# A transformer kernel with a planned instruction order: new start, new bias matmuls, own buffer tag, a modelled store latency of 4 instead of 8

## Chip, cores, metric

One core of a Trainium2 chip (trn2). The metric is the device time of one execution in microseconds; quoted times are medians over several executions.

## The reference

Two layers; each is a local attention block and a feed-forward block, with the same weights in both layers. Input is 2048 tokens of width 1024, in bf16.

```python
for layer in (1, 2):
    x = x + A(layernorm(x), wqkv, wo)      # 32 heads of 32; each token attends to itself and 7 earlier ones, 2 apart
    x = x + B(layernorm(x), w1, b1, w2, b2)
# B: h = relu(x @ w1 + b1)**2, width 3584;  h @ w2 + b2
```

## The kernel before

The tokens of each layer are processed as four units of 512, so there are units 0 to 7. A unit goes through these stages (names of tiles in brackets): layernorm to a transposed, normalised input (`xnA`); projections q, k, v (`pq`); attention, mostly on VectorE (products `P`, logits `lg` on TensorE, exponentials `e`, denominator `dn`, result `o`); output projection (`py`), residual (`xm`), second layernorm (`xnB`); feed-forward 1 and 2. Units 1 to 7 do the two feed-forward products with a Strassen-type scheme of 7 products instead of 8: feed-forward 1 as 256-wide matmuls into `X`, `Y`, `Z`, feed-forward 2 as 512-wide ones. It needs sums and differences of weight blocks. Unit 0 does its products plainly, forms these combinations on VectorE on the side (tiles `tv`) and stores them in DRAM (`w1s`, `tw`) for the others.

No instruction is issued where the program text stands. Every operation is put into a plan with a modelled duration, a priority and its dependencies; a list scheduler runs the plan against modelled engines, buffer classes and a modelled DMA rate, and the order in which it starts operations is the fixed order of each engine's queue.

```python
LAT, PE_SLACK, DMA_LAT, DMA_MBS = 0.25, 0.3, 2.2, 0.36      # the model's constants
class Plan:
    def schedule(self):
        # ... an operation is picked when its engine is free, its inputs are done, and for every new buffer
        # a slot of its class is free and the number of live buffers of that tag is under its cap:
        if b.tag in self.caps and (live.get(b.tag, 0) >= self.caps[b.tag] or b.idx != placed.get(b.tag, 0)):
            ok = False
        # ... a DMA ends at max(dma_free, end) + MB / DMA_MBS, plus op.lat
p.caps.update(w=5, xnA=1, xnB=1, tv=4, T=1, ...)             # one xnA alive at a time

def SA(self, u):                                             # load x, layernorm, transpose
    xnT = Buf("8K", "xnA", [128, 4, self.KD, 128], F16)
    after = [self.state[u - 2].get("gatev")] if u >= 2 else ()
    ...
def keep_w2(self, j0, n, w):                                 # combinations of w2, stored for units 1..7
    p.add("DVE", ..., 45.0, name="tv")
    self.dma(..., prio=50.0, name="twst", lat=8.0)           # keep_w1 likewise
def SW(self, u):                                             # output projection, residual, second layernorm
    ... self.ln(xm, ..., vec=False, on_pe=(u in (0, self.NU - 1)))    # vec: statistics on VectorE
def SF2(self, u):                                            # seven products; b2 is added by matmul, 2 per product:
    mul("B21", *block(1, 0), Y, True, 0); ... mul("T1", ..., Z, True, 1); ... mul("T4", *block(1, 1), X, False, 0)
```

The softmax here doesn't subtract the row's maximum and nothing guards it: scores larger than these inputs give would overflow.

Of the kernel before, what the change touches and what calls it, by code (L numbers as in the profile page):

```python
# [8 lines left out]
BF = mybir.dt.bfloat16  # L9
# [16 lines left out]
DMA_LAT = 2.2  # L26
DMA_MBS = 0.36


def dve(n, fast=True):  # L30
    return 0.15 + n * (0.000523 if fast else 0.00104)
# [177 lines left out]
class _Kernel:  # L209
# [19 lines left out]
    def setup(self):  # L229
# [22 lines left out]
        with nc.allow_non_contiguous_dma(reason="tiny bias load"):  # L252
            nc.gpsimd.dma_start(self.b1T[:], self.b1.rearrange("(c p) -> p c", p=128))
        self.b2r = const.tile([128, D], BF, name="b2r")
        nc.gpsimd.dma_start(self.b2r[:], self.b2.rearrange("(o d) -> o d", o=1).to_broadcast((128, D)))
        self.row0 = const.tile([128, 128], F16, name="row0")
        nc.vector.memset(self.row0[:], 1.0)
        nc.gpsimd.affine_select(out=self.row0[:], in_=self.row0[:], pattern=[[0, 128]], compare_op=ALU.is_equal,
                                fill=0.0, base=0, channel_multiplier=1)

# [24 lines left out]
        p.classes["ps"] = (8, 2048)  # L285
        p.caps.update(w=5, xt=2, P0=4, P1=4, pr=2, pb=2, dn=1, e=1, xm=6, xnA=1, xnB=1, xn=2, xo=2, q=1, k=1, v=1, o=1, r2=1, s1=1, tv=4, T=1, wl=2)

# [34 lines left out]
    def keep_w2(self, j0, n, w):  # L322
        nc, p = self.nc, self.p
        t = [Buf("2K", "tv", [128, 2, BLK], F16) for _ in range(4)]

        def raw(k2, n2):
            return w[:, k2, :n, n2 * BLK:(n2 + 1) * BLK]

        def comb(i, a, b, r):
            p.add("DVE", dve(n * BLK), lambda: nc.vector.tensor_tensor(t[i][:, :n], a(), b(), ALU.subtract), r, [(t[i], 0)], 45.0, name="tv")  # L330
            self.dma(lambda: self.tw[i][:, j0:j0 + n, :], lambda: t[i][:, :n], [(t[i], 0)], [(("tw", i), j0)], n * 0.13, prio=50.0, name="twst", lat=8.0)
        comb(0, lambda: raw(0, 1), lambda: raw(0, 0), [(w, 0)])
        comb(1, lambda: raw(1, 1), lambda: t[0][:, :n], [(w, 1), (t[0], 0)])
        comb(2, lambda: raw(1, 1), lambda: raw(0, 1), [(w, 0), (w, 1)])
        comb(3, lambda: raw(1, 0), lambda: t[1][:, :n], [(w, 1), (t[1], 0)])
# [30 lines left out]
    def add_b2(self, bank, n2, start):  # L366
        self.nc.tensor.matmul(bank[:], self.row0[:], self.b2r[:, n2 * BLK:(n2 + 1) * BLK], start=start, stop=False, skip_group_check=True)

# [34 lines left out]
    def keep_w1(self, dp, w):  # L403
        nc, p = self.nc, self.p
        at = {pr: i for i, (d, pr) in enumerate(self.order1) if d == dp}

        def raw(m, k):
            return w[:, m, 4 * k:4 * k + 4, :]

        def store(pr, src, r, cast=None):  # L410
            i = at[pr]
            self.dma(lambda: self.w1s[i // 4][:, i % 4], src, r, [(("w1s", i // 4), i % 4)], 0.26, prio=50.0, name="w1st", cast=cast, lat=8.0)
        s1, s3, s2, s4 = t = [Buf("2K", "tv", [128, 4, 256], F16) for _ in range(4)]

        def comb(t, a, b, op, r, pr):
            p.add("DVE", dve(1024), lambda: nc.vector.tensor_tensor(t[:], a(), b(), op), r, [(t, 0)], 45.0, name="tv")
            store(pr, lambda: t[:], [(t, 0)])
        comb(s1, lambda: raw(1, 0), lambda: raw(1, 1), ALU.add, [(w, 1)], 5)
        comb(s3, lambda: raw(0, 0), lambda: raw(1, 0), ALU.subtract, [(w, 0), (w, 1)], 7)
        comb(s2, lambda: s1[:], lambda: raw(0, 0), ALU.subtract, [(w, 0), (s1, 0)], 6)  # L420
        comb(s4, lambda: raw(0, 1), lambda: s2[:], ALU.subtract, [(w, 0), (s2, 0)], 3)
# [76 lines left out]
    def ln_first(self, x, xv, xnT, tl):  # L498
# [3 lines left out]
        st = Buf("H", "st", [128, D // 512, nc.vector.BN_STATS_DIM], F32)  # L502
        mv, lnv, rstd, nmr = (lambda: sm[:, 0:2]), (lambda: sm[:, 2:3]), (lambda: sm[:, 3:4]), (lambda: sm[:, 4:5])
        pr = self.nxt()
# [9 lines left out]

        def f3():
            nc.vector.scalar_tensor_tensor(out=nmr(), in0=sm[:, 0:1], scalar=-1.0, in1=rstd(), op0=ALU.mult, op1=ALU.mult)

        def f4():
            nc.scalar.activation(out=xn[:], in_=xv(), func=ACTF.Identity, bias=nmr(), scale=rstd())

        p.add("DVE", 1.6, f1, [(x, 0)], [(sm, 0), (st, 0)], -1e5 + pr, name="bn")
        p.add("ACT", 0.5, f2, [(sm, 0)], [(sm, 1)], -1e5 + pr, name="bn2")
        p.add("DVE", 0.15, f3, [(sm, 0), (sm, 1)], [(sm, 2)], -2e5 + pr, name="bn3")
        p.add("ACT", 1.05, f4, [(x, 0), (sm, 1), (sm, 2)], [(xn, 0)], -1e5 + pr, name="bn4")
        self.transpose(xn, xnT, tl, -1e5 + pr)

    def transpose(self, xn, xnT, tl, prio):
        nc, p, KD = self.nc, self.p, self.KD
        pt = Buf("ps", "pt", [128, KD, 128], F16)

        def f5():
            for kd in range(KD):
                nc.tensor.transpose(pt[:, kd, :], xn[:, kd * 128:(kd + 1) * 128], self.ident[:])

        def f6():
            nc.vector.tensor_copy(xnT[:, tl], pt[:])
        p.add("PE", 1.0, f5, [(xn, 0)], [(pt, 0)], prio, name="pt")
        p.add("DVE", 0.69, f6, [(pt, 0)], [(xnT, tl)], prio - 200.0, name="ptc")

# [11 lines left out]
    def SA(self, u):  # L551
        layer, b = divmod(u, self.NB)
        st = self.state.setdefault(u, {})
        xnT = Buf("8K", "xnA", [128, 4, self.KD, 128], F16)
        st["xnA"] = xnT
        after = [self.state[u - 2].get("gatev")] if u >= 2 else ()
        for tl in range(4):
# [7 lines left out]

    def SQ(self, u, jobs, order=None):
        nc, p = self.nc, self.p
# [22 lines left out]
        for nm, c0 in order:  # L590
# [3 lines left out]
            def fm(pq=pq, w=w, c0=c0):  # L594
                for kd in range(KD):
                    wv = w[kd // 4][:].rearrange("p (a b) n -> p a (b n)", a=4)
                    nc.tensor.matmul(pq[:], wv[:, kd % 4, c0:D:8], xnT[:, :, kd, :], start=(kd == 0), stop=(kd == KD - 1))  # L597
            st["gate" + nm] = self.pe(8, fm, [(xnT, i) for i in range(4)] + [(w[0], 0), (w[1], 0)], [(pq, 0)], name="pq")
            p.add("ACT", act(512), lambda dst=dst, c0=c0, off=off, pq=pq: nc.scalar.copy(dst[:, c0, off:off + BLK], pq[:]),  # L599
                  [(pq, 0)], [(dst, c0)], 2.0, name="cast")  # L600
            yield
# [106 lines left out]
    def SW(self, u):  # L708
# [8 lines left out]
        for tl in range(4):  # L717
# [3 lines left out]
            for db in range(D // 512):  # L721
# [7 lines left out]
                def fe(py=py, xm=xm, xv=xv, db=db):  # L729
# [4 lines left out]
            self.ln(xm, lambda xm=xm: xm[:], [0, 1], xnT, tl, lambda t=t: self.xnd[2 * layer + 1][t * 128:(t + 1) * 128, :],  # L734
                    (("xnd", 2 * layer + 1, t), 0), 1.0, False, on_pe=(u in (0, self.NU - 1)))

    def SF1_plain(self, u):
# [6 lines left out]
        for dp in range(self.NDP):  # L744
# [4 lines left out]
            for m in range(2):  # L749
                for a in range(2):  # L750
# [4 lines left out]
                    def fm(ph=ph, w=w, m=m, a=a):  # L755
                        for kd in range(KD):
                            nc.tensor.matmul(ph[:], w[:, m, kd, a * 128:(a + 1) * 128], xnT[:, :, kd, :], start=(kd == 0), stop=(kd == KD - 1))  # L757

                    def fr(ph=ph, r=r, f=f):
                        nc.scalar.activation(out=r[:], in_=ph[:], func=ACTF.Relu, bias=self.b1T[:, f:f + 1], scale=1.0)  # L760

                    def fs(r=r, f=f):
                        nc.scalar.activation(out=r2[:, f, :], in_=r[:], func=ACTF.Square)
                    self.pe(8, fm, [(xnT, i) for i in range(4)] + [(w, m)], [(ph, 0)], name="ph")
                    p.add("ACT", 0.69, fr, [(ph, 0)], [(r, 0)], 2.0, name="relu")
                    p.add("ACT", 0.63, fs, [(r, 0)], [(r2, (f, 0)), (r2, (f, 1))], 1.9, name="sq")
# [93 lines left out]
    def SF2(self, u):  # L860
# [35 lines left out]
        def block(k2, m2):  # L896
            return (lambda jj, q: r2[:, k2 * h + jj, m2 * HB + q * 128:m2 * HB + (q + 1) * 128]), (lambda j0: cells(k2, m2, j0))
# [9 lines left out]
        X, Y, Z = bank("X"), bank("Y"), bank("Z")  # L907
        mul("B11", *block(0, 0), X, True)
        for q in range(2):
            add(X[q], q, 0)  # L910
        for j0 in (0, g):
            comb(lambda j0=j0: blk(0, 0, j0), lambda j0=j0: s1[:, j0:j0 + g, :], lambda j0=j0: blk(0, 0, j0), ALU.subtract,
                 cells(0, 0, j0) + [(s1, j0)], cells(0, 0, j0))
        mul("B21", *block(1, 0), Y, True, 0)
        for q in range(2):
            self.out_tile(layer, b * 4 + q, 0, Y[q], xm[q])
        for j0 in (0, g):
            comb(lambda j0=j0: blk(1, 0, j0), lambda j0=j0: blk(1, 0, j0), lambda j0=j0: blk(0, 0, j0), ALU.subtract,
                 cells(1, 0, j0) + cells(0, 0, j0), cells(1, 0, j0))
        mul("T1", lambda jj, q: s1[:, jj, q * 128:(q + 1) * 128], lambda j0: [(s1, j0)], Z, True, 1)  # L920
        for q in range(2):
# [8 lines left out]
        for q in range(2):  # L930
            self.out_tile(layer, b * 4 + q, 1, Z[q], xm[q])
        mul("T4", *block(1, 1), X, False, 0)
        for q in range(2):
# [14 lines left out]
    def run(self, a, b=(), pace=1):  # L948
# [4 lines left out]
        for _ in b:  # L953
            pass

    def build(self):
        self.setup()
        NU = self.NU
        NCH = self.NCH
        self.SA(0)  # L960
        order = []
        for c0 in range(NCH - 2):
            order += [("k", c0), ("q", c0)]
        order += [("k", NCH - 2), ("k", NCH - 1), ("q", NCH - 2), ("q", NCH - 1)]
        self.run(self.SQ(0, "kq", order))
        self.run(self.SQ(0, "v"))
# [70 lines left out]
```

## Time and profile before

The five runs before the prediction had a median of 1237.2 us (1235.9 to 1240.0).

| | before |
|---|---|
| span of the profiled run | 1235.2 us |
| TensorE busy / VectorE busy | 1191.3 us (96%) / 1023.7 us (83%) |
| matmul work: all matmuls of the program at the spacing below | 1174.6 us |
| span up to the end of the last matmul, less that work | 57.1 us |
| of it before unit 1's feed-forward 1 (the "head") | 41.3 us |

Busy time is a poor gauge here. The Trainium skill ("Trainium Kernel Development and Optimization", Performance Expectations) says that matmul busy time is a bad metric because matmuls are pipelined. The trace agrees: matmuls 512 columns wide start 0.2157 us apart but each is recorded as 0.379 us long. So I count matmuls in the built program (0.2157 us for 512 columns, 0.109 for 256, 0.0558 for 128, the spacings of undisturbed stretches), and call what an interval takes beyond that count its *cost*: idle time, half-rate clock and pipeline ends.

From the page of before (busy time and share; busy tenths of 40 slices of 30.9 us; granted TensorE clock in tenths):

```profile
PE 1191.3 (96%) x6832; PEld 741.1 (60%) x6874; DVE 1023.7 (83%) x1553; ACT 676.5 (55%) x1240; POOL 4.3 (0%) x11
...
PE   6987999899999999999999999999999998999998
...
PEclk9998999999999999999999999999999999999999
```

Counted from 1, TensorE is busy for less than 90% of slices 1, 3, 4 and 8, all in the first 250 us, and of slices 34 and 40. The timeline of TensorE before shows the early gaps (start, duration, operation, matmuls in the group, and in brackets the idle time before it and what ended it):

```profile
14.25 7.36 PE L597 MATMUL pq<-xnA,w 128*128 128x512 f16 x20 [0.78 <-DVE xnA L536]
22.22 6.26 PE L597 MATMUL pq<-xnA,w 128*128 128x512 f16 x28 [0.61 <-DMA w<-in_A_wqkv_dram]
28.32 1.89 PE L645 MATMUL lg<-P,grp 128*128 128x512 f16 x8
...
88.67 12.05 PE L597 MATMUL pq<-xnA,w 128*128 128x512 f16 x48 [3.70 <-ACT k L599]
...
110.69 0.39 PE L726 MATMUL py<-w,o 128*128 128x512 bf16 x1 [1.77 <-DVE o L695]
113.34 4.02 PE L726 MATMUL py<-w,o 128*128 128x512 bf16 x9 [2.27 <-DVE o L695]
119.39 1.04 PE L533 MATMUL pt<-ident,xn 128*128 128x128 f16 x8 [2.03 <-ACT xn L450]
...
241.21 1.03 PE L597 MATMUL pq<-xnA,w 128*128 128x512 f16 x4
248.18 15.12 PE L597 MATMUL pq<-xnA,w 128*128 128x512 f16 x60 [5.95 <-DMA w<-in_A_wqkv_dram]
```

A group's duration also shows the clock. At full rate 9 matmuls take 9 x 0.2157 + 0.17 (the end of the last) = 2.1 us; at 113.34 they took 4.02, so the array ran at half rate after the wait. The long waits shown here, at 88, 110 to 120 and 248 us, are therefore each paid twice.

The wait at 88.67 names a cast on ScalarE (ACT), and ScalarE's own timeline shows why it was late: an operation that needs VectorE's denominator stood ahead of the casts in ScalarE's in-order queue.

```profile
87.28 0.42 ACT L675 ACTIVATE dn<-dn 128x256 f32<-128x256 f32 x1 [15.51 <-DVE dn L672]
87.73 0.42 ACT L676 ACTIVATE ri<-dn 128x256 bf16<-128x256 f32 x1
88.05 3.00 ACT L599 CAST k<-pq 128x512 f16<-128x512 f32 x6
```

The wait at 248.18 is a weight load. The timeline of the DMA-issuing queue (SP) shows that its second half was issued only at 240.96, just as TensorE got there, behind stores of combinations (`tw`) and results (`xs`):

```profile
231.50 0.40 SPq L302 DMA_DIRECT2D w<-in_A_wqkv_dram  x1
236.08 1.18 SPq L302 DMA_DIRECT2D xs<-xo  x2
...
239.34 1.52 SPq L302 DMA_DIRECT2D tw<-tv  x3
240.96 0.44 SPq L302 DMA_DIRECT2D w<-in_A_wqkv_dram  x1
```

### The profile page before, as it was taken

To read this page: it belongs to the slowest core of one execution; us is meant where nothing else is said; L and a number is where in the kernel's file an instruction comes from. 1 tells how busy PE (TensorE), PEld (TensorE's weight loads), DVE (VectorE), ACT (ScalarE), POOL (GpSimd) and SP (SyncE) were. 2 spreads that over 40 slices of the span, in tenths; PEclk is the share of its full clock that TensorE was granted. 3 is DMA by queue.
4 is the path that set the end of the run, shared out by engine and by line. 5 is a ranking of instruction groups with operands and counts; after the bars stand their busy time and mean duration, and the time that the engine had idled before them with its cause. 6 is when DMAs were issued, how large, how long until landed. Compare 5 with 4: busy or idle time off the path is not lost.

```text
span 1235.2 us, 17952 instructions
## 1 busy us (share of the span) xinstructions
PE 1191.3 (96%) x6832; PEld 741.1 (60%) x6874; DVE 1023.7 (83%) x1553; ACT 676.5 (55%) x1240; POOL 4.3 (0%) x11
## 2 busy tenths in 40 slices
PE   6987999899999999999999999999999998999998
PEld 3653544356855578456874658545784555844863
DVE  5799999837999899994989999894889999997562
ACT  6533895048851689119870488506982173752640
POOL 1000000000000000000000000000000000000000
PEclk9998999999999999999999999999999999999999
DMA  9685978798899688987989688897799946688964
GB/s 308 194 213 161 295 243 255 237 347 258 334 325 361 212 317 288 366 327 222 347 281 366 232 290 315 301 362 248 247 356 344 347 161 217 245 286 320 344 235 170
DMA packets 209239, 348.29 MB, mean 282 GB/s; under 512 B 67136, under 2 KB 133952, under 8 KB 196352
## 3 DMA queue, kind: packets, MB, share of 16 engines
q1 hardware_dynamic: 197984, 333.22, 79.9%
q10 hardware_dynamic: 7488, 13.63, 2.9%
q0 software_dynamic: 3680, 0.28, 0.5%
q8 instruction: 54, 0.88, 0.3%
q14 instruction: 33, 0.27, 0.1%
HBM read 292.56 MB, written 46.40 MB: 274 GB/s over the span
## 4 chain that ended last, share of the span: by engine, by line
PE 73%; DVE 16%; DMA 5%; ACT 4%; issue 1%; SPq 1%; ACTq 0%; DVEq 0%
PE pq L597 18%; PE X L833 13%; PE X L887 11%; PE Z L833 7%; PE Z L887 5%; PE py L726 5%; DVE pr L690 4%; PE py L358 4%; PE Y L833 3%; DMA w<-in_B_w_dram 3%; PE Y L887 2%; DMA w<-in_A_wqkv_dram 2%; DVE pr L693 2%; PE ph L757 2%; PE lg L645 2%; DVE pr L694 1%
## 5 line engine op out<-in xcount | busy, mean ns | idle before, releaser
L597 PE MATMUL pq<-xnA,w 128*128 128x512 f16 x1536 | 344.5, 384 | 11.0 <-DMA w<-in_A_wqkv_dram 6.6
L597 PEld LDWEIGHTS <-w 128*128 128x128 bf16 x1536 | 220.8, 144 | 130.4 <-issue 13.6
L833 PEld LDWEIGHTS <-w 128*128 128x128 f16 (+1 forms) x2544 | 248.9, 98 | 36.5 <-issue 1.5
L887 PEld LDWEIGHTS <-r 128*128 128x128 f16 x1176 | 114.8, 98 | 140.1 <-issue 5.8
L630 DVE TENSOR_TENSOR P<-q,k 128x2048 f16<-128x2048 f16 x128 | 152.7, 1223 | 51.5 <-ACT q L599 51.5
L887 PE MATMUL X<-w,r 128*128 128x512 f16 (+1 forms) x777 | 176.2, 379 | 1.3 <-DVE xm L893 1.0
L690 DVE TENSOR_TENSOR pr<-pb,v 128x2048 f16<-128x2048 f16 x128 | 156.5, 1223 | 1.0 <-DVE pb L679 0.5
L599 ACT CAST k<-pq 128x512 f16<-128x512 f32 x64 | 37.0, 588 | 196.1 <-PE pq L597 195.2
L833 PE MATMUL X<-T,w 128*128 128x256 f16 x1104 | 134.1, 273 | 1.3 <-ACT u L807 1.3
L638 DVE TENSOR_TENSOR P<-P,P 128x2048 f16<-128x2048 f16 x99 | 120.9, 1222 | 2.2
L726 PE MATMUL py<-w,o 128*128 128x512 bf16 x496 | 114.8, 386 | 5.0 <-DVE o L695 4.0
L821 ACT ACTIVATE r<-rr 128x1024 f16<-128x1024 f16 x98 | 102.0, 1057 | 10.2 <-DVE rr L817 8.1
L807 ACT CAST u<-X 128x512 f16<-128x512 f32 x147 | 83.9, 586 | 39.7 <-PE X L833 37.6
L693 DVE TENSOR_TENSOR pr<-pr 128x1024 f16<-128x1024 f16 x128 | 88.2, 689 | 3.1
L726 PEld LDWEIGHTS <-o 128*128 128x128 bf16 x512 | 50.8, 99 | 66.0 <-DVE o L695 4.8
L810 DVE TENSOR_TENSOR rr<-u,Z 128x512 f16<-128x512 f16 x98 | 65.6, 683 | 23.4 <-PE Z L833 14.2
L475 ACT ACTIVATE xn<-xm 128x1024 f16<-128x1024 f32 x32 | 33.9, 1058 | 80.9 <-DVE xm L731 72.4
L731 DVE TENSOR_TENSOR xm<-py,xt 128x512 f32<-128x512 f32 x64 | 43.4, 687 | 30.5 <-PE py L726 25.8
L675 ACT ACTIVATE dn<-dn 128x256 f32<-128x256 f32 x16 | 6.6, 416 | 109.1 <-DVE dn L672 108.7
L694 DVE TENSOR_TENSOR pr<-pr 128x512 f16<-128x512 f16 x128 | 54.4, 425 | 4.4
L817 DVE TENSOR_SCALAR rr<-rr,b1T 128x256 f16<-128x256 f16 (+1 forms) x196 | 51.0, 315 | 1.0
L358 PE MATMUL py<-w,r 128*128 128x512 bf16 x219 | 49.4, 379 | 0.3
(100 smaller groups left out, 1346.8 us busy)
## 6 DMA issues: line engine op xcount, KB each, us to landing
w<-w1s SPq DMA_DIRECT2D x78, 1024.0 KB, 8.7
w<-tw SPq DMA_DIRECT2D x56, 896.0 KB, 8.9
w<-in_A_wqkv_dram SPq DMA_DIRECT2D x48, 1024.0 KB, 8.5
w<-in_B_w_dram SPq DMA_DIRECT2D x42, 896.0 KB, 7.2
w<-in_A_wo_dram SPq DMA_DIRECT2D x16, 1024.0 KB, 8.5
xt<-xs SPq DMA_DIRECT2D x32, 512.0 KB, 8.7
w<-in_B_w_dram SPq DMA_DIRECT2D x28, 512.0 KB, 6.9
xs<-xo SPq DMA_DIRECT2D x32, 256.0 KB, 6.8
```

What stands on the lines that cost most here:

```text
L358: nc.tensor.matmul(bank[:], r2[:, k2 * h + j0 + j, tl * 128:(tl + 1) * 128], w[:, k2, j, n2 * BLK:(n2 + 1) * BLK], start=False, stop=(j0 + ...
L597: nc.tensor.matmul(pq[:], wv[:, kd % 4, c0:D:8], xnT[:, :, kd, :], start=(kd == 0), stop=(kd == KD - 1))
L630: nc.vector.tensor_tensor(cur[:], q[:, c, None, hb * HB:(hb + 1) * HB].to_broadcast([128, W, HB]), _win_ap(k[:, c, :], HALO + hb * HB, HB) ...
L638: nc.vector.tensor_tensor(other[:], other[:], cur[:], ALU.add)
L690: nc.vector.tensor_tensor(pr[:], pb[:], _win_ap(v[:, c, :], HALO + hb * HB, HB), ALU.mult)
L693: nc.vector.tensor_tensor(pr[:, 0:4, :], pr[:, 0:4, :], pr[:, 4:8, :], ALU.add)
L694: nc.vector.tensor_tensor(pr[:, 0:2, :], pr[:, 0:2, :], pr[:, 2:4, :], ALU.add)
L726: nc.tensor.matmul(py[:], o[:, c, tl * 128:(tl + 1) * 128], wos[c // 4][:].rearrange("p (a b) n -> p a (b n)", a=4)[:, c % 4, db * 512:(db ...
L807: p.add("ACT", act(512), lambda: nc.scalar.copy(us[i][:], X[:]), [(X, 0)], [(us[i], 0)], 1.0, name="u")
L821: p.add("ACT", act(1024), lambda: nc.scalar.activation(out=r2[:, f:f + 2, :].rearrange("p a t -> p (a t)"), in_=r[:].rearrange("p a m t -> ...
L833: nc.tensor.matmul(bank[:, a, :], lw[:, k, a * 128:(a + 1) * 128], rhs(k), start=(start and k == 0 and a == 0), stop=(k == 3), skip_group_ ...
L887: nc.tensor.matmul(banks[q][:], left(jj, q), w[:, j, :], start=(start and jj == 0 and b2 is None), stop=(jj == h - 1), skip_group_check=True)
```

## The change

Its intent is to fill TensorE's gaps in the head and to drop superfluous bias matmuls. It has seven parts; the names in capitals are mine. The diff is cut to its core.

```diff
 # RATE
-DMA_MBS = 0.36
+DMA_MBS = 0.38
 # B2: the b2 row enters through the product that feeds all four outputs, and a difference where needed
-        mul("B11", *block(0, 0), X, True)
+        mul("B11", *block(0, 0), X, True, 0)
-        mul("B21", *block(1, 0), Y, True, 0)
+        mul("B21", *block(1, 0), Y, True)
-        mul("T1", ..., Z, True, 1)
+        mul("T1", ..., Z, True, "d")
-        mul("T4", *block(1, 1), X, False, 0)
+        mul("T4", *block(1, 1), X, False)
+        # b2 as two rows, loaded, not broadcast to 128; selector matrices pick[0], pick[1], pick["d"]=pick[1]-pick[0]
 # CAP
-        p.caps.update(w=5, ...)
+        p.caps.update(pk=2, lg=4, w=5, ...)
 # STORE
-   keep_w2: self.dma(..., name="twst", lat=8.0)
+   keep_w2: self.dma(..., name="twst", lat=4.0)
-   keep_w1: self.dma(..., name="w1st", lat=8.0);  p.add("DVE", ..., 45.0, name="tv")
+   keep_w1: self.dma(..., name="w1st", lat=4.0);  p.add("DVE", ..., self.nxt(), name="tv")
 # START (ln_first, transpose, SQ of unit 0, build)
-            nc.scalar.activation(out=xn[:], in_=xv(), func=ACTF.Identity, bias=nmr(), scale=rstd())
+            nc.vector.tensor_scalar(out=xn[:], in0=xv(), scalar1=sm[:, 0:1], scalar2=rstd(), op0=ALU.subtract, op1=ALU.mult)
+        (nc.scalar.copy if act else nc.vector.tensor_copy)(xnT[:, tl], pt[:])     # act for two of four tiles
+            # the first 3 k projections as two 256-wide halves each, order k k k, then q and k in turn
+        self.keep_clock(11, self.p.ops[0])      # 11 dummy 512-wide matmuls (pk), lowest priority
 # TAG (SA)
-        xnT = Buf("8K", "xnA", [128, 4, self.KD, 128], F16)
+        xnT = Buf("8K", "xnA1" if u == 1 else "xnA", [128, 4, self.KD, 128], F16)
-        after = [self.state[u - 2].get("gatev")] if u >= 2 else ()
+        after = [self.state[max(u - 2, 1)].get("gatev")] if u >= 2 else ()
 # SPLIT (SW and plain feed-forward 1 of unit 0)
-     self.ln(xm, ..., False, on_pe=(u in (0, self.NU - 1)))
+     self.ln(xm, ..., u == 0 and tl >= 2, on_pe=(u in (0, self.NU - 1)))
+     # the first two ph outputs as two 256-wide halves each, the first needing only token tiles 0 and 1
```

More of the change, by code (lines that the diff above doesn't have):

```diff
@@ L253, in setup @@
             nc.gpsimd.dma_start(self.b1T[:], self.b1.rearrange("(c p) -> p c", p=128))
-        self.b2r = const.tile([128, D], BF, name="b2r")
-        nc.gpsimd.dma_start(self.b2r[:], self.b2.rearrange("(o d) -> o d", o=1).to_broadcast((128, D)))
-        self.row0 = const.tile([128, 128], F16, name="row0")
-        nc.vector.memset(self.row0[:], 1.0)
-        nc.gpsimd.affine_select(out=self.row0[:], in_=self.row0[:], pattern=[[0, 128]], compare_op=ALU.is_equal,
-                                fill=0.0, base=0, channel_multiplier=1)
+        self.b2r = const.tile([128, BLK], BF, name="b2r")
+        nc.vector.memset(self.b2r[:], 0.0)
+        for n2, row in enumerate((32, 0)):
+            nc.gpsimd.dma_start(self.b2r[row:row + 1, :], self.b2.rearrange("(o d) -> o d", o=1)[:, n2 * BLK:(n2 + 1) * BLK])
+        self.pick = {}
+        for n2, row in enumerate((32, 0)):
+            t = self.pick[n2] = const.tile([128, 128], BF, name=f"pick{n2}")
+            nc.vector.memset(t[:], 1.0)
+            nc.gpsimd.affine_select(out=t[:], in_=t[:], pattern=[[0, 128]], compare_op=ALU.is_equal,
+                                    fill=0.0, base=-row, channel_multiplier=1)
+        t = self.pick["d"] = const.tile([128, 128], BF, name="pickd")
+        nc.vector.tensor_tensor(t[:], self.pick[1][:], self.pick[0][:], ALU.subtract)
         self.wqkv_v = self.wqkv.rearrange("(kt p) n -> p kt n", p=128)
@@ L285, in setup @@
         p.classes["ps"] = (8, 2048)
-        p.caps.update(w=5, xt=2, P0=4, P1=4, pr=2, pb=2, dn=1, e=1, xm=6, xnA=1, xnB=1, xn=2, xo=2, q=1, k=1, v=1, o=1, r2=1, s1=1, tv=4, T=1, wl=2)
+        p.caps.update(pk=2, lg=4, w=5, xt=2, P0=4, P1=4, pr=2, pb=2, dn=1, e=1, xm=6, xnA=1, xnB=1, xn=2, xo=2, q=1, k=1, v=1, o=1, r2=1, s1=1, tv=4, T=1, wl=2)
     def place(self, b):
@@ L330, in comb @@
             p.add("DVE", dve(n * BLK), lambda: nc.vector.tensor_tensor(t[i][:, :n], a(), b(), ALU.subtract), r, [(t[i], 0)], 45.0, name="tv")
-            self.dma(lambda: self.tw[i][:, j0:j0 + n, :], lambda: t[i][:, :n], [(t[i], 0)], [(("tw", i), j0)], n * 0.13, prio=50.0, name="twst", lat=8.0)
+            self.dma(lambda: self.tw[i][:, j0:j0 + n, :], lambda: t[i][:, :n], [(t[i], 0)], [(("tw", i), j0)], n * 0.13, prio=50.0, name="twst", lat=4.0)
         comb(0, lambda: raw(0, 1), lambda: raw(0, 0), [(w, 0)])
@@ L366, in add_b2 @@
     def add_b2(self, bank, n2, start):
-        self.nc.tensor.matmul(bank[:], self.row0[:], self.b2r[:, n2 * BLK:(n2 + 1) * BLK], start=start, stop=False, skip_group_check=True)
+        self.nc.tensor.matmul(bank[:], self.pick[n2][:], self.b2r[:], start=start, stop=False, skip_group_check=True)
     def w2_rhs(self, name, half):
@@ L411, in store @@
             i = at[pr]
-            self.dma(lambda: self.w1s[i // 4][:, i % 4], src, r, [(("w1s", i // 4), i % 4)], 0.26, prio=50.0, name="w1st", cast=cast, lat=8.0)
+            self.dma(lambda: self.w1s[i // 4][:, i % 4], src, r, [(("w1s", i // 4), i % 4)], 0.26, prio=50.0, name="w1st", cast=cast, lat=4.0)
         s1, s3, s2, s4 = t = [Buf("2K", "tv", [128, 4, 256], F16) for _ in range(4)]
         def comb(t, a, b, op, r, pr):
-            p.add("DVE", dve(1024), lambda: nc.vector.tensor_tensor(t[:], a(), b(), op), r, [(t, 0)], 45.0, name="tv")
+            p.add("DVE", dve(1024), lambda: nc.vector.tensor_tensor(t[:], a(), b(), op), r, [(t, 0)], self.nxt(), name="tv")
             store(pr, lambda: t[:], [(t, 0)])
@@ L502, in ln_first @@
         st = Buf("H", "st", [128, D // 512, nc.vector.BN_STATS_DIM], F32)
-        mv, lnv, rstd, nmr = (lambda: sm[:, 0:2]), (lambda: sm[:, 2:3]), (lambda: sm[:, 3:4]), (lambda: sm[:, 4:5])
+        mv, lnv, rstd = (lambda: sm[:, 0:2]), (lambda: sm[:, 2:3]), (lambda: sm[:, 3:4])
         pr = self.nxt()
@@ L513, in f2, with transpose @@
             nc.scalar.activation(out=rstd(), in_=lnv(), func=ACTF.Exp, scale=-0.5)
-        def f3():
-            nc.vector.scalar_tensor_tensor(out=nmr(), in0=sm[:, 0:1], scalar=-1.0, in1=rstd(), op0=ALU.mult, op1=ALU.mult)
         def f4():
-            nc.scalar.activation(out=xn[:], in_=xv(), func=ACTF.Identity, bias=nmr(), scale=rstd())
-        p.add("DVE", 1.6, f1, [(x, 0)], [(sm, 0), (st, 0)], -1e5 + pr, name="bn")
-        p.add("ACT", 0.5, f2, [(sm, 0)], [(sm, 1)], -1e5 + pr, name="bn2")
-        p.add("DVE", 0.15, f3, [(sm, 0), (sm, 1)], [(sm, 2)], -2e5 + pr, name="bn3")
-        p.add("ACT", 1.05, f4, [(x, 0), (sm, 1), (sm, 2)], [(xn, 0)], -1e5 + pr, name="bn4")
-        self.transpose(xn, xnT, tl, -1e5 + pr)
-    def transpose(self, xn, xnT, tl, prio):
+            nc.vector.tensor_scalar(out=xn[:], in0=xv(), scalar1=sm[:, 0:1], scalar2=rstd(), op0=ALU.subtract, op1=ALU.mult)
+        p.add("DVE", 1.55, f1, [(x, 0)], [(sm, 0), (st, 0)], -1e5 + pr, name="bn")
+        p.add("ACT", 0.55, f2, [(sm, 0)], [(sm, 1)], -1e5 + pr, name="bn2")
+        p.add("DVE", 0.5, f4, [(x, 0), (sm, 0), (sm, 1)], [(xn, 0)], -2e5 + pr, name="bn4")
+        self.transpose(xn, xnT, tl, -1e5 + pr, act=tl % 2 == 0)
+    def transpose(self, xn, xnT, tl, prio, act=False):
         nc, p, KD = self.nc, self.p, self.KD
@@ L535, in f6 @@
         def f6():
-            nc.vector.tensor_copy(xnT[:, tl], pt[:])
+            (nc.scalar.copy if act else nc.vector.tensor_copy)(xnT[:, tl], pt[:])
         p.add("PE", 1.0, f5, [(xn, 0)], [(pt, 0)], prio, name="pt")
-        p.add("DVE", 0.69, f6, [(pt, 0)], [(xnT, tl)], prio - 200.0, name="ptc")
+        p.add("ACT" if act else "DVE", 1.05 if act else 0.69, f6, [(pt, 0)], [(xnT, tl)], prio - 200.0, name="ptc")
     def load_x(self, layer, t, after=(), prio=None, tag="xt"):
@@ L564, in SA, with SQ @@
                         (("xnd", 2 * layer, t), 0), 20.0, False)
-    def SQ(self, u, jobs, order=None):
+    def SQ(self, u, jobs, order=None, split=0):
         nc, p = self.nc, self.p
@@ L597, in fm, with fh @@
                     nc.tensor.matmul(pq[:], wv[:, kd % 4, c0:D:8], xnT[:, :, kd, :], start=(kd == 0), stop=(kd == KD - 1))
-            st["gate" + nm] = self.pe(8, fm, [(xnT, i) for i in range(4)] + [(w[0], 0), (w[1], 0)], [(pq, 0)], name="pq")
+            if split:
+                def fh(n2, pq=pq, w=w, c0=c0):
+                    for kd in range(KD):
+                        wv = w[kd // 4][:].rearrange("p (a b) n -> p a (b n)", a=4)
+                        nc.tensor.matmul(pq[:, n2 * HB:(n2 + 1) * HB], wv[:, kd % 4, c0:D:8], xnT[:, 2 * n2:2 * n2 + 2, kd, :],
+                                         start=(kd == 0 and n2 == 0), stop=(kd == KD - 1), skip_group_check=True)
+                for n2 in range(2):
+                    self.pe(4, lambda fh=fh, n2=n2: fh(n2), [(xnT, 2 * n2), (xnT, 2 * n2 + 1), (w[0], 0), (w[1], 0)], [(pq, n2)],
+                            prio=self.nxt() + 3.0 * n2, name="pq")
+                split -= 1
+            else:
+                st["gate" + nm] = self.pe(8, fm, [(xnT, i) for i in range(4)] + [(w[0], 0), (w[1], 0)], [(pq, 0), (pq, 1)], name="pq")
             p.add("ACT", act(512), lambda dst=dst, c0=c0, off=off, pq=pq: nc.scalar.copy(dst[:, c0, off:off + BLK], pq[:]),
-                  [(pq, 0)], [(dst, c0)], 2.0, name="cast")
+                  [(pq, 0), (pq, 1)], [(dst, c0)], 2.0, name="cast")
             yield
@@ L734, in SW @@
             self.ln(xm, lambda xm=xm: xm[:], [0, 1], xnT, tl, lambda t=t: self.xnd[2 * layer + 1][t * 128:(t + 1) * 128, :],
-                    (("xnd", 2 * layer + 1, t), 0), 1.0, False, on_pe=(u in (0, self.NU - 1)))
+                    (("xnd", 2 * layer + 1, t), 0), 1.0, u == 0 and tl >= 2, on_pe=(u in (0, self.NU - 1)))
     def SF1_plain(self, u):
@@ L757, in fm, with fh @@
                             nc.tensor.matmul(ph[:], w[:, m, kd, a * 128:(a + 1) * 128], xnT[:, :, kd, :], start=(kd == 0), stop=(kd == KD - 1))
+                    def fh(n2, ph=ph, w=w, m=m, a=a):
+                        for kd in range(KD):
+                            nc.tensor.matmul(ph[:, n2 * HB:(n2 + 1) * HB], w[:, m, kd, a * 128:(a + 1) * 128], xnT[:, 2 * n2:2 * n2 + 2, kd, :],
+                                             start=(kd == 0 and n2 == 0), stop=(kd == KD - 1), skip_group_check=True)
                     def fr(ph=ph, r=r, f=f):
@@ L763, in fs @@
                         nc.scalar.activation(out=r2[:, f, :], in_=r[:], func=ACTF.Square)
-                    self.pe(8, fm, [(xnT, i) for i in range(4)] + [(w, m)], [(ph, 0)], name="ph")
-                    p.add("ACT", 0.69, fr, [(ph, 0)], [(r, 0)], 2.0, name="relu")
+                    if dp or m:
+                        self.pe(8, fm, [(xnT, i) for i in range(4)] + [(w, m)], [(ph, 0), (ph, 1)], name="ph")
+                    else:
+                        for n2 in range(2):
+                            self.pe(4, lambda fh=fh, n2=n2: fh(n2), [(xnT, 2 * n2), (xnT, 2 * n2 + 1), (w, m)], [(ph, n2)], prio=self.nxt() + 4.0 * n2, name="ph")
+                    p.add("ACT", 0.69, fr, [(ph, 0), (ph, 1)], [(r, 0)], 2.0, name="relu")
                     p.add("ACT", 0.63, fs, [(r, 0)], [(r2, (f, 0)), (r2, (f, 1))], 1.9, name="sq")
@@ L919, in SF2 @@
                  cells(1, 0, j0) + cells(0, 0, j0), cells(1, 0, j0))
-        mul("T1", lambda jj, q: s1[:, jj, q * 128:(q + 1) * 128], lambda j0: [(s1, j0)], Z, True, 1)
+        mul("T1", lambda jj, q: s1[:, jj, q * 128:(q + 1) * 128], lambda j0: [(s1, j0)], Z, True, "d")
         for q in range(2):
@@ L954, in run, with keep_clock, fk @@
             pass
+    def keep_clock(self, n, after):
+        nc = self.nc
+        for _ in range(n):
+            pk = Buf("ps", "pk", [128, BLK], F32)
+            def fk(pk=pk):
+                g = self.grp[:].rearrange("p h r -> p (h r)")
+                nc.tensor.matmul(pk[:], g, g[:, None, :].to_broadcast([128, 4, 128]), start=True, stop=True)
+            self.p.add("PE", 0.43, fk, (), [(pk, 0)], 1e6, after=[after], name="pk")
     def build(self):
@@ L960, in build @@
         self.SA(0)
-        order = []
-        for c0 in range(NCH - 2):
-            order += [("k", c0), ("q", c0)]
-        order += [("k", NCH - 2), ("k", NCH - 1), ("q", NCH - 2), ("q", NCH - 1)]
-        self.run(self.SQ(0, "kq", order))
+        self.keep_clock(11, self.p.ops[0])
+        order = [("k", c0) for c0 in range(3)]
+        for c0 in range(3, NCH):
+            order += [("q", c0 - 3), ("k", c0)]
+        order += [("q", c0) for c0 in range(NCH - 3, NCH)]
+        self.run(self.SQ(0, "kq", order, 3))
         self.run(self.SQ(0, "v"))
```

## The prediction

> **What bounds the kernel now.** TensorE. The page gives PE 96% busy (1191.3 us of 1235.2), DVE 83%; the chain of waits is 73% PE. The program's matmuls at the spacing the timeline shows (0.2157 us for 512 columns, 0.109 for 256) make about 1175 us; some 60 us is PE idle, cold clock and drain. The PE timeline puts most of it in the first 250 us:
> - start: 10.6 us idle in all, and projections spaced 0.43 us until 20.15, about 3 us lost to a cold clock;
> - 3.7 us at 85-88.7 (ACT sits 15.5 us behind a wait for the softmax denominator, k casts queue behind it, PE runs out of PSUM banks), then about 1.7 us cold;
> - 6.3 us at 109-120 (output projection waits for DVE's attention, then ACT's layernorm), then about 3.6 us cold;
> - 0.7 us at 140-143;
> - 5.9 us at 242-248 (wqkv load issued only at 240.96, behind stores), then about 2.2 us cold.
> Later gaps total about 10 us, the tail 3.5.
>
> **What the change does.**
> 1. b2 enters the seven Strassen-type blocks with 4 matmuls, not 6: 14 fewer, 14 x 0.2157 = 3.0 us, all on the PE path.
> 2. Start: 11 dummy matmuls warm the clock; the normalise goes to DVE, two copies to ACT, the first projections are split in halves. But the second half of the k weights lands at about 15.5 us and the q weights at 22.2, and the built order needs q after 28 matmuls (6.0 us). The start is load-bound: worth 2-2.5 us.
> 3. Built order: 11 unit-1 casts now precede the second denominator op on ACT: the 3.7+1.7 us go.
> 4. Unit 0's output projection is split around v projections (six units, 10.4 us of filler), w1 combinations no longer jump ahead of attention on DVE, two layernorms get their statistics on DVE: most of 6.3+3.6 us goes.
> 5. The wqkv loads are issued before the xs stores: the 5.9+2.2 us go.
>
> Sum: 3.0+2.5+5.4+9.9+0.7+8.1 = 29.6 us, the ceiling. Against it: DVE is over 95% busy from 61 to 232 us, and gets 16 more w2 combinations (0.68 us each), eight evictions and about 3 us of bn_stats before unit 1's attention ends. I estimate that end at about 250 us; an unhindered PE needs it at about 247. DMA share there, 0.83 on average, rises too. I keep 75-80% of the head gain, 21 us, plus 3. Units 2-7 keep their structure; their waits are reshuffled, not removed.
>
> **Predicted: 1213 us; 8 in 10 between 1205 and 1224.** Faster by over 2%: 0.46; within 2%: 0.53; slower: 0.01.
>
> **The Trainium skill**, "TensorE: Matmul & The Clock Gate", Part 1, says an idle array runs at half rate until about 3.4 us of activity; the trace agrees on the rate (0.43 against 0.216 us). Part 4 says transposes don't count as busy; the trace fits: transposes from 8.18 us, yet the clock rises 5.9 us after projections begin at 14.25.
>
> **What would show it.** First k projections near 15 us spaced 0.216, first q waiting for weights near 22; no PE idle over 1 us at 70-125 us; the gap near 240 gone or turned into a wait of the output projection on DVE's o; b2 matmuls 50 -> 36; granted clock in the slices of 62-124 us up from 0.94 and 0.83 to 1.
>
> **What would make it wrong.** A new DVE or DMA wait at 220-260 us that eats half the gain (about 1222); a new in-order block on ACT or the DMA queue, where transposes now stand before v's weights; the clock falling back between dummies and projections; or later waits improving too (about 1205).

## The result, and the profile after

| | before | after |
|---|---|---|
| median | 1238.2 us (15 runs) | 1219.5 us (8 runs, 1217.4 to 1221.7) |
| ratio of the means, 95% interval | | 0.985 (0.984 to 0.986) |
| span of the profiled run | 1235.2 us | 1217.3 us |
| TensorE busy | 1191.3 us | 1184.3 us |
| matmul work without dummies | 1174.6 us | 1171.6 us |
| cost of the head (dummies counted as cost) | 41.3 us | 23.2 us |
| cost of the rest | 15.8 us | 18.9 us |

A ratio is the mean time of one kernel's runs over that of the other's in the same rounds, so it is not quite the ratio of the medians. The gain of 18.7 us is far outside the noise. The last three rows add up: 3.0 + 18.1 - 3.1 = 18.0 us, against 17.9 between the spans. TensorE's busy time fell by only 7.0 us. All outputs are right.

The page after, same lines:

```profile
PE 1184.3 (97%) x6867; PEld 743.6 (61%) x6911; DVE 1026.1 (84%) x1562; ACT 669.8 (55%) x1226; POOL 5.0 (0%) x13
...
PE   6999899999999999999999999999999999999998
...
PEclk9999899999999999999999999999999999999999
```

The gaps of slices 3, 4, 8 and 34 are gone. Slice 5 (122 to 152 us) has taken a new one, with a lower clock. TensorE's timeline after:

```profile
12.60 0.66 PE L604 MATMUL pq<-xnA,w 128*128 128x256 f16 x4 [1.35 <-DMA w<-in_A_wqkv_dram]
15.79 1.07 PE L604 MATMUL pq<-xnA,w 128*128 128x256 f16 x4 [2.53 <-DMA w<-in_A_wqkv_dram]
16.66 1.06 PE L535 MATMUL pt<-ident,xn 128*128 128x128 f16 x8
17.51 4.39 PE L604 MATMUL pq<-xnA,w 128*128 128x256 f16 x32
...
94.26 7.07 PE L739 MATMUL py<-w,o 128*128 128x512 bf16 x31
101.17 3.62 PE L599 MATMUL pq<-xnA,w 128*128 128x512 f16 x16
...
114.61 7.07 PE L739 MATMUL py<-w,o 128*128 128x512 bf16 x31
...
128.30 1.03 PE L535 MATMUL pt<-ident,xn 128*128 128x128 f16 x8 [2.58 <-ACT xn L456]
130.65 3.57 PE L770 MATMUL ph<-xnB,w 128*128 128x512 f16 x8 [1.31 <-DVE xnB L538]
...
231.38 13.98 PE L599 MATMUL pq<-xnA,w 128*128 128x512 f16 x64
...
346.89 3.17 PE L909 MATMUL X<-w,r 128*128 128x512 f16 x7 [2.40 <-DMA w<-tw]
```

Read from top to bottom. The array, warmed by the dummies, runs 4 half-width matmuls in 0.66 us at 12.60, waits 2.53 us for the second half of the k weights, and is at half rate again at 15.79 (1.07 us for the same work). The output projection is in two pieces with v projections between them and has no wait. But the transposes of the third and fourth layernorm now wait (128.30), and the 8 matmuls at 130.65 take 3.57 us instead of 1.9: half rate. The 64 projections at 231.38 have no wait; the second half of their load was issued 22 us ahead:

```profile
209.40 0.38 SPq L308 DMA_DIRECT2D w<-in_A_wqkv_dram  x1
```

At 346.89, in unit 1, there is a wait that before did not have, again with a half-rate stretch behind it (7 matmuls in 3.17 us).

### The profile page after: what moved, and what is told of

Read it like the earlier page. It is cut to its first block, busy times and chain, and to the rows that moved or that the text cites. A ratio compares the mean times of both kernels' runs of the same rounds, so it can differ in the third digit from the quotient of the medians.

```text
span 1217.3 us, 18017 instructions
## 1 busy us (share of the span) xinstructions
PE 1184.3 (97%) x6867; PEld 743.6 (61%) x6911; DVE 1026.1 (84%) x1562; ACT 669.8 (55%) x1226; POOL 5.0 (0%) x13
## 4 chain that ended last, share of the span: by engine, by line
PE 80%; DVE 10%; DMA 6%; ACT 2%; issue 1%; SPq 0%; ACTq 0%; DVEq 0%
PE pq L599 21%; PE X L855 13%; PE X L909 12%; PE py L739 7%; PE Z L855 7%; PE Z L909 6%; PE py L364 4%; PE Y L855 3%; DMA w<-in_B_w_dram 3%; PE Y L909 2%; DVE pr L703 2%; PE ph L770 2%; PE lg L658 2%; DMA w1s<-tv 1%; DVE pr L706 1%; DVE P L643 1%
## 5 line engine op out<-in xcount | busy, mean ns | idle before, releaser
L599 PE MATMUL pq<-xnA,w 128*128 128x512 f16 x1512 | 332.2, 379 | 0.0
L599 PEld LDWEIGHTS <-w 128*128 128x128 bf16 x1512 | 216.7, 144 | 110.2
L739 PE MATMUL py<-w,o 128*128 128x512 bf16 x496 | 112.1, 379 | 0.8
L871 ACT ACTIVATE rr<-X,b1T 128x256 f16<-128x256 f32 x98 | 41.3, 471 | 17.0 <-PE X L855 16.9
```

Source lines behind the costliest of these rows:

```text
L599: nc.tensor.matmul(pq[:], wv[:, kd % 4, c0:D:8], xnT[:, :, kd, :], start=(kd == 0), stop=(kd == KD - 1))
L739: nc.tensor.matmul(py[:], o[:, c, tl * 128:(tl + 1) * 128], wos[c // 4][:].rearrange("p (a b) n -> p a (b n)", a=4)[:, c % 4, db * 512:(db ...
```

## The experiments

The parts were put on *before* one at a time or taken from *after* one at a time. For each kernel the cost of the head and of the rest was taken from its trace as above (dummies counted as cost):

| kernel | median us | ratio to before, 95% interval | head cost | rest cost |
|---|---|---|---|---|
| before | 1238.2 to 1239.7 | 1 | 41.3 | 15.8 |
| after | 1219.5 | 0.9850 (0.9840, 0.9861) | 23.2 | 18.9 |
| only_b2 | 1235.5 | 0.9969 (0.9956, 0.9981) | 41.8 | 16.5 |
| only_xna1 | 1240.7 | 1.0014 (0.9993, 1.0034) | 40.0 | 18.5 |
| only_store | 1230.8 | 0.9930 (0.9915, 0.9945) | 31.3 | 19.7 |
| only_start | 1242.5 | 1.0030 (1.0012, 1.0047) | 41.2 | 20.7 |
| no_xna1 | 1227.1 | 0.9899 (0.9878, 0.9921) | 31.1 | 19.0 |
| no_start | 1215.8 | 0.9806 (0.9789, 0.9824) | 21.9 | 17.2 |
| no_split | 1222.0 | 0.9857 (0.9840, 0.9875) | 27.7 | 17.7 |
| no_mbs | 1216.8 | 0.9815 (0.9794, 0.9835) | 21.3 | 16.5 |
| no_pk | 1218.9 | 0.9843 (0.9828, 0.9858) | 23.8 | 18.3 |
| ln_dve | 1225.3 | 0.9898 (0.9882, 0.9915) | 23.2 | 24.0 |
| no_start_mbs | 1216.5 | 0.9836 (0.9806, 0.9867) | 23.2 | 17.1 |
| three_parts | 1224.2 | 0.9877 (0.9859, 0.9896) | 28.3 | 21.6 |

Two cautions. The experiments ran in four sets of rounds, each on another chip, so compare them by their ratios to before, not by their medians. And each cost comes from one trace, while the runs of one kernel differ by 0.5 to 8 us (before: 1235.9 to 1242.6 over all rounds); the profiled run of no_mbs lies 2.2 us below its median, that of three_parts 2.5 us above. A difference in cost of 1 or 2 us is therefore an indication and not a result. The fences below show only the core of each edit.

### One part alone

**only_b2** is before plus B2.

```diff
-        mul("B21", *block(1, 0), Y, True, 0) ... mul("T1", ..., 1) ... mul("T4", ..., 0)
+        mul("B11", *block(0, 0), X, True, 0) ... mul("T1", ..., "d")
```

> Before plus the b2 part alone (4 instead of 6 bias matmuls in each of the seven blocks, bias rows loaded instead of broadcast). The built order of everything else is unchanged. Theory: the 14 matmuls lie on the PE path, 14 x 0.2157 = 3.0 us, so about 1235.2 against 1238.2, ratio 0.9976; excess over matmul work unchanged. Rival: joins with DVE and loads absorb it, under 1 us.

Measured: 1235.5 us, 3.0 us below before's 1238.5 in the same rounds. The work fell by 3.0 us (14 matmuls), and the cost moved by 1.2 us. The theory holds: here the matmuls removed were time removed, and the interval of the ratio, 2.4 to 5.4 us, leaves out the rival. One sentence of the expectation was too wide: built again without a run, only_b2's order equals before's only up to the modelled time of 357 us, which covers the head, and differs after it.

**only_xna1** is before plus TAG.

```diff
-        xnT = Buf("8K", "xnA", ...)
+        xnT = Buf("8K", "xnA1" if u == 1 else "xnA", ...)
```

> Before plus the two lines in SA alone: a tag of its own for unit 1's normalised input, and the gate of unit 2's x loads. In the built order 34 casts instead of 26 then stand before the second denominator op on ACT, and unit 0's output projection is split around v projections. Theory: this alone takes away the ACT block (3.7 idle + 1.7 cold) and most of the output projection's waits (6.3 + 3.6 with the cold clock), so 9 to 15 us, about 1223 to 1229; the wait for the wqkv load near 240 stays at 4 to 8 us. Rival: DVE bounds the head, and what PE gains is handed back at that wait or at the next output projection: gain under 4 us.

Measured: 1240.7 us, no gain. My theory fell and the rival's size holds; that VectorE is what bounds the head was not shown by it. The order did change as expected and the wait behind the ScalarE queue is gone, but the timeline of TensorE in only_xna1 shows other waits in its place:

```profile
106.31 0.62 PE L533 MATMUL pt<-ident,xn 128*128 128x128 f16 x8 [3.23 <-ACT xn L450]
...
133.76 1.03 PE L533 MATMUL pt<-ident,xn 128*128 128x128 f16 x8 [4.09 <-ACT xn L450]
136.06 4.13 PE L757 MATMUL ph<-xnB,w 128*128 128x512 f16 x12 [1.27 <-DVE xnB L536]
...
246.32 4.07 PE L597 MATMUL pq<-xnA,w 128*128 128x512 f16 x9 [7.70 <-DMA w<-in_A_wqkv_dram]
```

TensorE comes to the projections of unit 2 3.6 us earlier (237.6 against 241.2 us) and waits 1.75 us longer for the same late load: part of the gain is handed back there, the other part never came, because the layernorms are late.

**only_store** is before plus STORE.

```diff
-            self.dma(..., name="twst", lat=8.0)
+            self.dma(..., name="twst", lat=4.0)
```

> Before plus the store part alone (modelled store latency 4 instead of 8, the w1 combinations in program order). In the built order the wqkv loads of unit 2 then stand before all xs stores. Theory: it removes the wait of 5.9 us and the 2.2 us cold after it near 240, and little else: about 1230. Rival: it is DMA or DVE that bounds there, and the wait moves to the output projection: gain under 3 us.

Measured: 1230.8 us, a head cost of 31.3 against 41.3. The theory holds. The wait near 240 us is gone; the same group starts at 239.32 without idle time:

```profile
224.64 14.84 PE L358 MATMUL py<-w,r 128*128 128x512 bf16 x68
239.32 5.99 PE L597 MATMUL pq<-xnA,w 128*128 128x512 f16 x27
```

The two edits of STORE were also built apart, without a run: the new latency alone puts the wqkv loads ahead of all xs stores in the built order, the new priority alone does not. As I read the plan, at most four `tv` may be alive (`tv=4`), and one comes free only when its store has ended in the model; a shorter modelled store lets the combinations, and the weight loads behind them, come earlier. No operation changed, and the median fell by 7.7 us. It is not shown that 4.0 is the truer number: from issue to landing the `tw` and `w1s` stores took a median of 2.9 and 4.3 us in before, but 6.0 and 6.3 in only_store and 5.7 and 6.8 in after.

**only_start** is before plus START.

```diff
+        self.keep_clock(11, self.p.ops[0])
+        # normalise on DVE, two copies on ACT, 3 k projections in halves, k before q
```

> Before plus the start alone (dummy matmuls, normalise on DVE, split first projections, k before q). Theory: the start is bound by the loads of the k and q weights, worth 2 to 2.5 us, about 1236. Rival: it is worth the cold clock and the earlier first tile, 5 to 6 us, about 1232.5.

Measured: 1242.5 us, 4 us slower. Neither expectation fits. The head's cost is unchanged (41.2), and the rest costs 4.9 us more, in stages whose operations START does not touch.

### One part removed

**no_xna1** is after without TAG.

```diff
-        xnT = Buf("8K", "xnA1" if u == 1 else "xnA", ...)
+        xnT = Buf("8K", "xnA", ...)
```

> After without the two lines in SA. In the built order 27 casts, not 35, stand before the second denominator op on ACT, and 56 matmuls of unit 0's output projection come in one piece. Theory (the parts only work together: the rename makes filler placeable, the other parts bring the layernorm in time to use it): the ACT block of 3 to 4 us and the output projection's waits come back, 8 to 12 us slower than after, about 1228 to 1231, with the excess before SF2_plain up from 20.6 to about 30. Rival (the rename is worth what it was worth alone, nothing): within 2 us of after, about 1219.

Measured: 1227.1 us, head cost 31.1 against 23.2. The timeline of TensorE in no_xna1 has the wait for ScalarE's casts back, and those of the output projection (0.86 and 2.26 us on `o`, then 3.50 us):

```profile
90.43 10.41 PE L599 MATMUL pq<-xnA,w 128*128 128x512 f16 x40 [2.92 <-ACT k L612]
...
119.90 0.62 PE L535 MATMUL pt<-ident,xn 128*128 128x128 f16 x8 [3.50 <-ACT xn L456]
```

The theory holds, with a total (7.6 us by the medians, 6.1 by the ratios) somewhat under its 8 to 12 us: the rename that is worth 1.3 us in the head alone is worth 7.9 us in company.

**no_start** is after without START.

```diff
-        self.keep_clock(11, self.p.ops[0])
-        # and the rest of START
```

> After without the start part. Theory: the start alone made before 4 us slower through later stages, not through the start itself; its own worth in the excess before the first FFN is 2 to 3 us, so the head's excess rises by 2 to 3 us and the total by about 2, less the 2.4 us of dummy matmuls that are then no work: 1220 to 1222. Rival: the start is a loss in the whole as well, about 1215.

Measured: 1215.8 us; the interval of its ratio lies wholly below after's, so it beats both kernels. The rival is right in the total, yet not in its place. Count what TensorE has done when the first logit matmul starts. No_start reaches it at 28.05 us with 12.1 us of work done, a cost of 15.9; after at 29.51 with 13.9 us done, a cost of 15.6; before at 28.3 with 12.1 us done, a cost of 16.2. So START gains 0.3 to 0.6 us where it acts, which is too little to be sure of from one trace each, and the loss of about 3 us arises later: 1.3 us in what follows in the head and 1.7 in the rest (23.2 and 18.9 against 21.9 and 17.2). The wait of unit 1 on `tw`, for one, is absent in no_start.

**no_split** is after without SPLIT.

```diff
-     self.ln(xm, ..., u == 0 and tl >= 2, ...)
+     self.ln(xm, ..., False, ...)
```

> After without DVE statistics for the last two layernorms of unit 0's output projection and without the half-width first FFN matmuls. Theory: these bring the third and fourth layernorm forward; without them the wait of the transposes on ACT (2.6 us and 1.3 us on the copy in after) becomes 5 to 8 us and the excess before SF2_plain rises by 3 to 6 us, about 1224. Rival: the DVE round trip costs as much as it saves: within 1.5 us of after.

Measured: 1222.0 us, and the head costs 4.5 us more, with waits of 2.30, 4.09 and 1.78 us where after has 2.58 and 1.31. The theory holds for the head. In total no_split is not told apart from after: by the ratios it is 0.9 us slower and the intervals overlap, so there the rival's "within 1.5 us" stands as well; 1.2 us came back in the rest.

**no_mbs** is after without RATE.

```diff
-DMA_MBS = 0.38
+DMA_MBS = 0.36
```

> After with the planner's modelled DMA rate back at 0.36: no operation changes, only the order in which independent ones are issued. Theory (the new wait of unit 1 on a stored-weight load, 2.4 us and 1.7 us cold, excess +6.0, is an accident of order, not a cost of the change): the head keeps its gain within 2 us, and the excess of units 1 to 7, 19.1 in after and 24.0 in before, moves by up to 5 us either way and the wait on tw in unit 1 is gone or elsewhere. Rival (the faster head makes the loads of unit 1 late whatever the order): the same wait stands within 1 us at the same place.

Measured: 1216.8 us. No operation differs from after, and the interval of the ratio lies below after's. In the trace, which is a fast one, the head costs 1.9 us less and the rest 2.4 us less. The order of products in unit 1 is another one, and the wait on `tw` is not there; the corresponding stretch of TensorE's timeline in no_mbs has 0.29 us of idle time:

```profile
338.94 3.19 PE L909 MATMUL X<-w,r 128*128 128x512 bf16 x14
342.41 0.38 PE L373 MATMUL Z<-b2r,pickd 128*128 128x512 bf16 x1 [0.29 <-DVE xo L963]
```

The theory holds: that wait was an accident of the planned order.

**no_pk** is after without the dummy matmuls alone.

```diff
-        self.keep_clock(11, self.p.ops[0])
```

> After without the 11 dummy matmuls, the rest of the start part kept. Theory: the dummies buy no time at the start, because the wait of 2.5 us for the second half of the k weights lets the clock fall back and the q weights bound the start anyway: the first attention-logit matmul (29.5 us in after) comes within 0.8 us of that, while the first projections run at the half rate somewhat longer. Later stages are re-ordered by the planner and may differ by several us for reasons of their own. Rival: the dummies save their purpose, a cold clock of 3 us: first logit matmul at about 32.5 us.

Measured: 1218.9 us, not told apart from after. TensorE's timeline at the start of no_pk:

```profile
12.50 1.07 PE L604 MATMUL pq<-xnA,w 128*128 128x256 f16 x4 [0.45 <-DMA w<-in_A_wqkv_dram]
15.64 1.08 PE L604 MATMUL pq<-xnA,w 128*128 128x256 f16 x4 [2.06 <-DMA w<-in_A_wqkv_dram]
...
17.36 4.95 PE L604 MATMUL pq<-xnA,w 128*128 128x256 f16 x32
...
29.93 1.03 PE L658 MATMUL lg<-P,grp 128*128 128x512 f16 x4
```

The first logit matmul comes at 29.93 us instead of 29.51. The dummies buy 0.4 us, not 3: the same weight load holds both up until 15.6 to 15.8 us, and the clock they raised falls back in that wait. The theory holds.

### What was left, and combinations

**ln_dve** goes after the wait at 128 us in after: one VectorE operation normalises, instead of VectorE, then ScalarE.

```diff
-            p.add("DVE", 0.1, g3, ...)        # minus mean times rstd
-            p.add("ACT", 1.25, f3, ...)       # normalise
+            p.add("DVE", 0.7, gn, ...)        # tensor_scalar: subtract mean, times rstd
```

> After with the third and fourth layernorm of unit 0's output projection normalised by one DVE op (subtract, multiply) instead of DVE for minus-mean-times-rstd and then ACT. Theory: what remains of the wait at 125 to 131 us in after (2.6 + 1.3 us idle and about 2.5 us of cold clock) is this DVE-ACT round trip through two in-order queues; without it the excess between the first FFN matmul and SF2_plain falls from 7.0 by 3 to 5 us. Rival: the transposes wait for the output projection and its eviction themselves: that excess stays within 1.5 us of 7.0.

Measured: 1225.3 us, 6 us worse than after. The wait for the transposes fell from 2.58 to 1.56 us, but the wait for the copy rose from 1.31 to 1.80, and the cost of that stretch only from 7.0 to 6.5. So the round trip was not what bound, as the rival had it (within 1.5 us of 7.0). VectorE's timeline in ln_dve shows its queue without a gap there, and the normalise and the copy standing behind attention products:

```profile
124.43 0.69 DVE L466 BATCH_NORM_STATS2 bs<-xm 128x6 f32<-128x512 f32 x1
125.15 0.21 DVE L475 BATCH_NORM_AGGREGATE sm<-bs 128x2 f32<-128x12 f32 x1
125.27 1.18 DVE L642 TENSOR_TENSOR P<-q,k 128x2048 f16<-128x2048 f16 x1
126.37 0.81 DVE L474 TENSOR_SCALAR xn<-xm,sm 128x1024 f16<-128x1024 f32 x1
```

That VectorE's load bounds this stretch is how I read it; no run tested it. The loss is in the rest (24.0 against 18.9), in units 2, 3, 4 and 7 (3.0, 1.2, 1.6 and 4.9 us more, with 4.6 less in unit 1), which the edit does not touch.

**no_start_mbs** takes both START and RATE from after.

```diff
-DMA_MBS = 0.38
+DMA_MBS = 0.36
-        # START
```

> After without the start part and with the planner's DMA rate back at 0.36. Each alone gained about 3 us on after. Theory (both gains are redraws of the order of later stages, not costs of the two edits): they do not add; the result lies anywhere from 1212 to 1220, with the head's excess within 3 us of the 21.9 of after without the start. Rival (each is a true cost of its own): they add, about 1213.

Measured: 1216.5 us (one of four runs at 1223.9 widens the interval). The two gains do not add, as the theory had it: together they would give a ratio near 0.977, and the interval begins at 0.9806.

**three_parts** is before plus B2, STORE and TAG.

```diff
-lat=8.0; "xnA"; six b2 matmuls per block
+lat=4.0; "xnA1" for unit 1; four b2 matmuls per block
```

> Before plus three parts: the b2 part, the store part, and the two lines in SA; no start part, no DVE statistics, no half-width matmuls, planner's rate 0.36. The head's excess (idle, cold and drain before unit 1's first FFN matmul) was 41.3 us in before, 40.0 with the two SA lines alone, 31.4 with the store part alone, 21.9 with all but the start part. Theory (what the two SA lines gain was handed back at the wqkv load, and the store part takes that wait away): the head's excess is 25 to 28 us, 4 to 6 us below the store part alone, and the time 1219 to 1224. Rival (the SA lines need the DVE statistics and half-width matmuls to be worth anything): the excess stays at 30 to 32 and the time at 1227 to 1229.

Measured: 1224.2 us with a head cost of 28.3, each just outside the theory's window and far from the rival's. With STORE in place TAG, together with B2, is worth 3.0 us in the head (31.3 to 28.3) against 1.3 for TAG alone. The step from 28.3 to no_start_mbs's 23.2 comes from SPLIT and CAP, the last 1.3 us to no_start's 21.9 from RATE. No run tests CAP, but without it (`lg=4` left out of after and the plan built, not run) the order is the same up to the modelled time of 1006 us, so in the head the step is SPLIT's. RATE's sign is not fixed: it gains 1.3 us there without START and costs 1.9 with it, both within the caution under the table.

## Why the prediction was right, and where its sum was off

The range held; the middle did not: 24 us of gain were forecast, 18.7 came. That the range held owes something to luck: the prediction took 20 to 25% off the head's gain for a wait on VectorE or DMA near 250 us that did not come, and this allowance covered most of what was lost at the start and in the layernorm chain instead. Point by point:

- **b2, 3.0 us: right.** The bias matmuls went from 50 to 36 in the profile, and the part alone gained 3.0.
- **Start, "worth 2-2.5 us": mis-sized.** It was worth 0.3 to 0.6. The step that failed is in the text itself: I named "the clock falling back between dummies and projections" as a risk and still counted the first 28 matmuls at full rate (6.0 us). From 15.79 us they ran at half rate until about 19 us, and after had done its first 20 matmuls' worth at 21.7 us, as before had. The q weights did not bind in after at all; "first q waiting for weights near 22" was wrong.
- **"The 3.7+1.7 us go": right**, but through the TAG lines, which I read only as a fact of the built order. Alone they gave almost nothing.
- **"Most of 6.3+3.6 us goes": the step that failed most.** With the 0.7 us after it, this stretch cost 10.6 us in before. In after, 4.1 us of waits and about 2.6 us of half rate (from the group durations at 128 to 136 us) are back some 10 us later, at the transposes and copies of the same layernorms: 3.9 us gained, not 9 to 10. I had looked at what fills TensorE while it waits for `o`, and not at the chain behind it (evict, statistics, normalise, transpose, copy), which no filler shortens. only_xna1 shows that chain with nothing to soften it.
- **"The 5.9+2.2 us go": right**, at 8.0, and STORE alone does it.
- The feared new wait on VectorE's attention near 250 us did not appear, narrowly: unit 1's last `o` ended at 254.4 us, and the second piece of its output projection started at 255.6. (A reading of before behind this fear was a little high: VectorE is busy 94% from 61 to 232 us, not over 95%.)
- **"Units 2-7 keep their structure; their waits are reshuffled": right in kind, but unit 1 was left out.** It got a new wait of 2.4 us and 1.7 us of half rate, and its cost went up by 5.9 us; units 2 to 7 cost 2.8 us less. Net: a loss of 3.1 us.

The head: 0.6 + 5.4 + 3.9 + 8.0 = 17.9 us, against 18.1 measured; with 3.0 for b2 and 3.1 lost in the rest, the 18 us.

On the rest: over the fourteen kernels of the table, whose later stages do the same work except for the b2 matmuls, the rest cost 15.8 to 24.0 us. Every edit whose plan was compared (B2, STORE, RATE and those of no_pk and ln_dve) redraws the order from some point on. For RATE, which changes no operation, the redraw is the only cause there can be; that it is also why START alone and ln_dve lose is likely, as their losses lie in units that they do not touch, but no run shows it. What stays open is which of these orders is good for a reason; only the wait of unit 1 was shown to be an accident.

On the clock: the Trainium skill ("TensorE: Matmul & The Clock Gate", Part 1) gives half rate for an idle array, and the traces agree (0.43 us against 0.216 per matmul).

## What to carry to other kernels

Where a list scheduler fixes the order, judge an edit by the stage it touches, from the trace, and treat the change of the total as that plus a redraw of several microseconds elsewhere; try neighbouring orders before a part is called a gain or a loss. Changing one modelled latency, with one priority, was worth more here (7.7 us) than any other part that was run alone. Filling one wait shows its worth only when the next wait in the chain is taken away too, so test parts both alone and by removal.

## What the Trainium skill lacked or had wrong

- "TensorE: Matmul & The Clock Gate", table "Why this matters for your kernels", advises no TensorE idle gaps above about 3 us. Shorter ones cost the clock here: after 2.40 us (after, 346.89 us: 7 matmuls in 3.17 us) and after 2.04 us (only_store, 778.68 us) the array was at half rate, while after 2.70 us (no_split, 351.23 us) it was not, nor after 3.23 us (only_xna1, 106.31 us: 8 transposes in 0.62 us). So the length of the wait alone does not decide it in these traces. The lines of only_store and of no_split, each from its timeline of TensorE (that of after is shown above):

```profile
778.68 3.04 PE L887 MATMUL Y<-w,r 128*128 128x512 bf16 x7 [2.04 <-DMA w<-in_B_w_dram]
```

```profile
351.23 1.69 PE L900 MATMUL X<-w,r 128*128 128x512 f16 x7 [2.70 <-DMA w<-tw]
```

- The same page, Part 4, says that the full clock does not engage for transposes. That they don't raise it fits no_pk: transposes from 7.19 us, projections still at half rate at 15.64. But they run faster when it is up: 8 transposes took 0.61 us behind the dummies in after and 1.03 us without them in no_pk.
- No page treats dummy matmuls that wake the array inside a kernel. Here 11 of them bought 0.4 us (no_pk), because a load wait of 2.53 us followed, after which the array was at half rate again.
- No page treats the spread that a re-drawn static order brings to untouched stages: 15.8 to 24.0 us of cost here.
